# A fused attention and two-MLP kernel: the softplus table's place, B and C stored without zeros, and an early order planned with eight transfers in flight

## The chip, the cores and the metric

One core of one Trainium2 chip runs the program. The metric is device time in microseconds (us), the median of three runs. Engines: PE is TensorE (matmuls), ACT ScalarE, DVE VectorE, POOL GpSimd; SP is SyncE, which here only issues transfers (its queue is SPq).

## The reference

Three stages follow each other. Stage 1 is a linear attention with decay (4 sequences, 8 heads, 768 positions, head size 32, state size 16):

```python
log_a = np.log(np.clip(a, 1e-06, 1.0))
cum = np.cumsum(la, axis=-1)                       # per chunk
M = einsum(C, B) * exp(cum_i - cum_j) * causal
y = M @ x + (C @ state) * exp(cum)
state = decay_full * state + sum_j B_j x_j decay_from_j
```

Stage 2 (MLP 1) and stage 3 (MLP 2) each take 3072 tokens of 256 features through 2048 hidden features and back:

```python
h = x @ w_in
g = np.maximum(h, 0.0) + np.log1p(np.exp(-np.abs(h)))      # stage 2: softplus
g = np.where(h >= 1, h, np.where(h <= -1, 0, (h + 1)**2/4)) # stage 3
out = (g @ w_out).astype(np.float32)
```

The MLP weights come as 64-bit floats and are put together from their 32-bit halves on the chip.

## The kernel before

**Tiling.** The 768 positions are six blocks of 128 (c = 0 to 5). A block of all four sequences (b = 0 to 3) gives 512 tokens. An MLP step s is one `up(s)` (128 hidden features for 512 tokens, in a PSUM bank h or z), the activation `g(s)` and one `down(s)` (into two accumulators). The first four steps do block 0 in halves: 256 tokens and two feature groups each. Precise products are made of a high part and a low part of each factor: `up` is six matmuls (`wih` with `xh`, `wil` with `xh`, `wih` with `xl`, for two halves of the 256 features). A `down` of the first WHOLE = 8 steps takes `g` and the 32-bit weight `w32` undivided; later ones take `g_hi`, `g_lo` and split weights (`woh`, `wol`) in six matmuls.

**The way of a weight.** A weight piece (kind i or o, number j; 512 KB) is loaded into a staging buffer `st0` to `st3`, or, for j = 2, `raw` (`load_w`, L780). From its two halves it is made: `w0` (the upper half, scaled; on ACT, or DVE), `w1` (the lower half's bits, on ACT with Relu), `w2` and, for weights whose sign `w0` hasn't taken, `w3` (both on DVE). PRELU says how many i and o pieces get their sign in `w0`, by a Prelu on ACT. `w_hi` casts to `wih` or `woh`, `split_w` (L966) makes `wil` or `wol` on DVE or POOL.

**Attention, block 0.** ACT makes eight exponentials (`decay`, L1125), POOL the products `bt` (`sources`, L1131), PE the `scores` of B and C (L1170), DVE `weigh` (L1179), PE `out` for each sequence (L1236, L1257), ACT and DVE `xh` and `xl` (`evac` L1289, `ready` L1297). `up(0)` and `up(1)` need sequences 0 and 1, `up(2)` and `up(3)` the other two.

**B and C.** A pair of sequences of a block comes as one tile `bc` of 128 x 768 numbers (384 KB), a third B and two thirds C; half of the C part is zeros, so that one matmul gives two heads apart.

**What sets the order.** `Jobs.order` is a planner: each job has an engine, a cost, needs and buffers; the planner takes jobs one by one by start and due time, and the code is written out in that order. Every engine then does its instructions strictly in that order, each waiting for what it needs. ACT holds one table of functions at a time: exp, ln and Prelu first, softplus after a table load, which stands inside `g(0)` at L1421. Where the planner sees PE idle in the first 26 us, matmuls on a tile of zeros are put in (L1545, "idle"); LULL = 5 of them stand before `down(0)`. In SP's queue each issue also waits until the eighth one before it has landed, so no more than eight transfers are in flight.

Of the kernel before, what the change touches and what calls it, by code (L numbers as in the profile page):

```python
# [15 lines left out]
Q = 128  # L16
# [11 lines left out]
class Jobs:  # L28
# [18 lines left out]
    def order(self, slots, begin):  # L47
# [29 lines left out]
        pipe = 0.0  # L77
# [23 lines left out]
        for _ in range(len(jobs)):  # L101
# [142 lines left out]
def program():  # L244
# [23 lines left out]
    add("clip_a", DVE, 380, needs=["a_load"])  # L268
    add("log", ACT, 260, needs=["clip_a"])
# [6 lines left out]
    add("clip_load", SP, 400, due=-1e5, size=98e3)  # L276
    add("clip", DVE, 350, needs=["clip_load", ("columns", 1)] + [("rows_of", b) for b in range(NB - 1)])
# [3 lines left out]
    for c in range(1, NC):  # L281
        add(("store_runs", c), ACT if c == 1 else SP, 450 if c == 1 else 600, needs=[("runs", 1)], size=16e3)
        add(("dec", c), ACT if c == 1 else SP, 600 if c == 1 else 400, needs=[("store_runs", i) for i in range(1, NC if c > 1 else 2)], takes=["dec"], size=262e3)
    for u in range(NU):
        c, b = divmod(u, NB)
        if u % 2 == 0:
            add(("load_bc", u // 2), SP, 400, takes=["bc"], size=393e3)
        add(("load", u), SP, 400, takes=["u"], size=262e3)
# [162 lines left out]
    for s, (m, c, t0, n, fc, m_fc) in enumerate(steps):  # L451
# [30 lines left out]
        if m == 0:  # L482

            add(
                ("g", s), ACT, 500 if s else 1850, needs=[made] + [("decay", b, hg) for b in range(NB * (s == 0)) for hg in range(2)]
                + [("w0", 0, kind, j) for kind in "io" for j in range(8 * (s == 0)) if signed(0, kind, j)],
# [37 lines left out]
    result = jobs.order(slots, {POOL: 3700, ACT: 2000, PE: 5500, DVE: 2500, SP: 900})  # L524
# [6 lines left out]
WHOLE = 8  # L531
# [16 lines left out]
PRELU = (2, 2)  # L548
LOW_ACT = 1
LOW_DVE = set()  # L550
PRE_FROM = 3
BIAS = {DVE: 400, POOL: 500}
# [25 lines left out]
    ("cd", 7): -1000, ("decay", 5): -16000, ("load_w", 1, "i", 2): -16000, ("w1", 0, "o", 1): 16000, ("weigh", 2, 0): -16000,  # L578
}
WARM = 10  # L580
LULL = 5
# [6 lines left out]
def tile_kernel(ctx: ExitStack, tc: tile.TileContext, a0, al, bc, ub, w_in, w_out, w2_in, w2_out, out):  # L588
# [486 lines left out]
    def load_bc(engine, v):  # L1075

        nc.sync.dma_start(mine("load_bc", v)[0], bc[v])
# [521 lines left out]
```

## Time and profile before

| | |
|---|---|
| runs | 555.07, 555.45, 555.97 us (median 555.45) |
| the profiled execution | 555.7 us, of which its span is 553.9 us |
| PE busy | 547.3 us, 99% of the span |
| DVE, ACT, POOL busy | 437.5, 391.1, 38.8 us |
| moved by DMA | 64.73 MB |

The profile's times run from the span's start. A row of the timeline gives the start and the duration of an instruction, or of several alike that are merged, and in brackets how long its engine sat idle before it, and what ended that. Instructions of one engine overlap a little at their ends, so the distance of two starts is often shorter than a duration.

### The profile page before, as it was taken

To read this page: it belongs to the slowest core of one execution; us is meant where nothing else is said; L and a number is where in the kernel's file an instruction comes from. 1 tells how busy PE (TensorE), PEld (TensorE's weight loads), DVE (VectorE), ACT (ScalarE), POOL (GpSimd) and SP (SyncE) were. 2 spreads that over 40 slices of the span, in tenths; PEclk is the share of its full clock that TensorE was granted. 3 is DMA by queue.
4 is the path that set the end of the run, shared out by engine and by line. 5 is a ranking of instruction groups with operands and counts; after the bars stand their busy time and mean duration, and the time that the engine had idled before them with its cause. 6 is when DMAs were issued, how large, how long until landed. Compare 5 with 4: busy or idle time off the path is not lost.

```text
span 553.9 us, 10465 instructions
## 1 busy us (share of the span) xinstructions
PE 547.3 (99%) x4001; PEld 442.8 (80%) x4001; DVE 437.5 (79%) x817; ACT 391.1 (71%) x719; POOL 38.8 (7%) x44
## 2 busy tenths in 40 slices
PE   9999999999999999999999999999999999999997
PEld 4777878888888888888888888888888888888885
DVE  7889899798856899876687898989886665876663
ACT  7969655636456667665666989786988875988783
POOL 4023110000000100001300000021310000000000
PEclk9999999999999999999999999999999999999999
DMA  7996458567232500376337324514100001100002
GB/s 271 392 238 198 130 179 235 165 213 219 90 133 76 181 1 1 113 253 227 111 116 233 108 77 145 179 38 149 44 1 0 2 0 38 39 0 1 1 1 76
DMA packets 34679, 64.73 MB, mean 117 GB/s; under 512 B 3684, under 2 KB 8164, under 8 KB 34628
## 3 DMA queue, kind: packets, MB, share of 16 engines
q1 hardware_dynamic: 34276, 63.65, 35.8%
q8 instruction: 31, 0.51, 0.4%
q10 hardware_dynamic: 352, 0.41, 0.3%
q14 instruction: 20, 0.16, 0.1%
HBM read 47.61 MB, written 16.43 MB: 116 GB/s over the span
## 4 chain that ended last, share of the span: by engine, by line
PE 93%; DMA 2%; DVE 2%; ACT 1%; SPq 1%; issue 1%; DVEq 0%; ACTq 0%
PE acc L1463 45%; PE h L1334 5%; PE h L1335 5%; PE h L1336 5%; PE z L1334 4%; PE z L1335 4%; PE z L1336 4%; PE h L1327 4%; PE h L1329 4%; PE h L1328 4%; PE acc L1451 3%; PE y L1236 1%; DMA st<-in_w_in_dram 1%; PE y L1268 1%; DMA u<-in_ub_dram 1%; PE z L1329 1%
## 5 line engine op out<-in xcount | busy, mean ns | idle before, releaser
L1437 DVE TENSOR_TENSOR gl<-g,gh 128x512 fp32r<-128x512 f32 x182 | 127.5, 705 | 55.0 <-PE acc L1463 31.1
L1463 PE MATMUL acc<-gh,woh 128*128 128x512 f32 x368 | 144.3, 392 | 0.0
L1463 PE MATMUL acc<-gh,wol 128*128 128x512 f32 x368 | 143.3, 389 | 0.0
L733 ACT CAST gh<-g 128x512 fp32r<-128x512 f32 x171 | 106.2, 621 | 26.4 <-PE acc L1463 14.2
L1463 PE MATMUL acc<-gl,woh 128*128 128x512 f32 x368 | 113.5, 389 | 0.0
L1463 PEld LDWEIGHTS acc<-gh,woh 128*128 128x128 f32 x368 | 69.1, 188 | 15.3 <-issue 0.7
L1463 PEld LDWEIGHTS acc<-gl,woh 128*128 128x128 f32 x368 | 69.1, 188 | 14.4
L1463 PEld LDWEIGHTS acc<-gh,wol 128*128 128x128 f32 x368 | 69.1, 188 | 14.1
L1422 ACT ACTIVATE g<-h 128x512 f32<-128x512 f32 x61 | 36.5, 598 | 52.5 <-PE h L1329 36.6
L1414 ACT ACTIVATE t<-t 128x512 f32<-128x512 f32 x96 | 60.9, 634 | 1.9
L1327 PE MATMUL h<-xh,wih 128*128 128x512 f32 (+1 forms) x114 | 45.8, 402 | 0.0
L1328 PE MATMUL h<-xh,wil 128*128 128x512 f32 (+1 forms) x114 | 42.8, 376 | 0.0
L1329 PE MATMUL h<-xl,wih 128*128 128x512 f32 (+1 forms) x114 | 42.8, 376 | 0.0
L1123 DVE TENSOR_TENSOR_SCAN ld<-ld,eye_t 128x512 f32<-128x512 f32 x20 | 26.5, 1364 | 2.2 <-DMA ld<-clip_z 2.2
L1407 ACT ACTIVATE t<-h 128x512 f32<-128x512 f32 x37 | 22.1, 598 | 7.5 <-PE h L1336 6.5
L1426 DVE TENSOR_TENSOR g<-h,t 128x512 f32<-128x512 f32 x37 | 25.3, 685 | 1.1 <-ACT t L1414 0.3
L1407 ACT ACTIVATE t<-z 128x512 f32<-128x512 f32 x35 | 21.0, 599 | 7.1 <-DVE g L1426 3.9
L1327 PEld LDWEIGHTS h<-xh,wih 128*128 128x128 f32 x114 | 21.5, 188 | 5.3 <-issue 1.1
L1426 DVE TENSOR_TENSOR g<-z,t 128x512 f32<-128x512 f32 x35 | 24.0, 686 | 1.5 <-ACT t L1414 0.5
L1328 PEld LDWEIGHTS h<-xh,wil 128*128 128x128 f32 x114 | 21.4, 188 | 4.6 <-issue 0.7
L1329 PEld LDWEIGHTS h<-xl,wih 128*128 128x128 f32 x114 | 21.4, 188 | 4.1
L1422 ACT ACTIVATE g<-z 128x512 f32<-128x512 f32 x19 | 11.4, 598 | 17.0 <-PE z L1336 8.5
(326 smaller groups left out, 1011.5 us busy)
## 6 DMA issues: line engine op xcount, KB each, us to landing
st<-in_w_in_dram SPq DMA_DIRECT2D x15, 512.0 KB, 5.2
st<-in_w_out_dram SPq DMA_DIRECT2D x15, 512.0 KB, 6.3
u<-in_ub_dram SPq DMA_DIRECT2D x24, 256.0 KB, 6.6
ld<-clip_z SPq DMA_DIRECT2D x20, 256.0 KB, 6.2
bc<-in_bc_dram SPq DMA_DIRECT2D x12, 384.0 KB, 5.7
pre_i<-st_plain SPq DMA_DIRECT2D x15, 256.0 KB, 2.0
pre_s<-st_plain SPq DMA_DIRECT2D x14, 192.0 KB, 5.9
pre_o<-st_plain SPq DMA_DIRECT2D x10, 256.0 KB, 2.5
```

Of the source, the lines that this page charges most:

```text
L733: nc.scalar.copy(out, in_)
L1327: nc.tensor.matmul(o, wh, xh[c][:, k, t0:t0 + n], start=(k == 0), stop=False)
L1328: nc.tensor.matmul(o, wl, xh[c][:, k, t0:t0 + n], start=False, stop=False)
L1329: nc.tensor.matmul(o, wh, xl[c][:, k, t0:t0 + n], start=False, stop=(k == 1))
L1334: nc.tensor.matmul(bank, wh, bh, start=start, stop=False, skip_group_check=True)
L1335: nc.tensor.matmul(bank, wl, bh, start=False, stop=False, skip_group_check=True)
L1336: nc.tensor.matmul(bank, wh, bl, start=False, stop=True, skip_group_check=True)
L1414: nc.scalar.activation(out=t, in_=t, func=AF.Square, scale=0.5 / SAT, bias=0.5)
L1422: nc.scalar.activation(out=g, in_=ph, func=AF.Softplus)
L1426: nc.vector.tensor_tensor(out=g, in0=ph, in1=t, op=ALU.max)
L1437: engines[engine].tensor_tensor(out=mine("g_lo", s)[0], in0=mine("g", s)[0], in1=mine("g_hi", s)[0].bitcast(F32), op=ALU.subtract)
L1463: nc.tensor.matmul(acc_t(s, e), w, g[:, j * n:(j + 1) * n], start=(begins(e, j) and g is gh and i == 0), stop=(fc + j == NFC - 1 and g is ...
```

## The change

- `table` becomes a job of its own. It needs block 0's eight exponentials and the Prelu weights, and no longer stands inside `g(0)`.
- B and C of a pair of sequences are stored as 128 rows of 512 numbers, in two halves by row parity, with no zeros. Two transfers of 64 x 512 load them, each into the columns where its rows have data. The places of the zeros in the three `bc` buffers are cleared once (`clear`: two on DVE, one on POOL). The matmuls of `scores` read the same columns in a strided way.
- The planner holds SP until the eighth transfer back has landed. Costs of a few jobs are set anew, and so are numbers that steer the order.
- PRELU (2, 2) becomes (2, 1): piece (o, 1) gets its sign by `w3`. Eight `w1` move from ACT to DVE (LOW_DVE). WHOLE 8 becomes 7, LULL 5 becomes 1.

```diff
+                lands += [end + self.LATENCY[SP]] * (2 if cost >= 800 else 1)
+                clock[SP] = max([clock[SP]] + lands[-8:-7])
...
+    add("table", ACT, 1280, needs=[("decay", b, hg) for b in range(NB) for hg in range(2)]
+        + [("w0", 0, kind, j) for kind in "io" for j in range(8) if signed(0, kind, j)])
...
-            add(("load_bc", u // 2), SP, 400, takes=["bc"], size=393e3)
+            add(("load_bc", u // 2), SP, 800, takes=["bc"], size=262e3 if u else 170e3)
...
-                ("g", s), ACT, 500 if s else 1850, needs=[made] + ...
+                ("g", s), ACT, 500, needs=[made] + ["table"] * (s == 0),
...
-WHOLE = 8
+WHOLE = 7
-PRELU = (2, 2)
+PRELU = (2, 1)
-LOW_DVE = set()
+LOW_DVE = {(0, 'i', 6), (0, 'i', 2), (0, 'i', 5), (0, 'o', 7), (0, 'i', 7), (0, 'o', 0), (0, 'o', 6), (0, 'i', 0)}
-BIAS = {DVE: 400, POOL: 500}
+BIAS = {DVE: 300, POOL: 500}
-LULL = 5
+LULL = 1
...
     def load_bc(engine, v):
-        nc.sync.dma_start(mine("load_bc", v)[0], bc[v])
+        t = mine("load_bc", v)[0].rearrange("(r e) f -> e r f", e=2)
+        for e in range(2):
+            nc.sync.dma_start(t[e][:, 256 * e:256 * e + 512], bc[v, e])
...
+    def table(engine):
+        nc.scalar.preload_act_table_set("softplus")
...
+    def clear(engine, i):
+        engine.memset(buf("bc", i).rearrange("r (k f) -> r k f", k=3)[:, 0:3:2], 0.0)
```

**ACT from the first `s0` copy to `g(0)`.** `w32<-st1` is `w0` of weight (o, 0), `st2` holds (i, 1), `st3` (o, 1); `t<-` and `g<-` are `w1`; `gh<-h1` is `g(0)`. Before:

```order
L1289 CAST xh0_360<-y1_266 128x2x128
L1291 COPY s0_66<-y1_266 128x64
L794 ACTIVATE w32_383<-st1_137 128x512
L804 ACTIVATE t_387<-st1_137,low_bias_73 128x512
L794 ACTIVATE w32_327<-st2_138 128x512
L804 ACTIVATE t_406<-st3_139,low_bias_73 128x512
L794 ACTIVATE w32_383<-st3_139 128x512
L804 ACTIVATE g_412<-st2_138,low_bias_73 128x512
L1421 ACT_TABLE_LOAD
L1422 ACTIVATE gh_415<-h1_210 128x512
```

Now, the same stretch of ACT:

```order
L797 ACTIVATE w32_368<-st1_137 128x512
L736 CAST wih0_74<-w32_331 128x512
L1294 CAST xh0_362<-y1_267 128x2x128
L1296 COPY s0_66<-y1_267 128x64
L797 ACTIVATE w32_331<-st2_138 128x512
L807 ACTIVATE t_392<-st2_138,low_bias_73 128x512
L1423 ACT_TABLE_LOAD
L807 ACTIVATE t_431<-st3_139,low_bias_73 128x512
L1429 ACTIVATE gh_434<-h1_212 128x512
```

One ACT instruction on `st3` instead of two stands ahead of `g(0)`, and it stands behind the table load; the cast of `wih0` has come to ACT, ahead of sequence 1's `xh0`.

**SP's queue at the start.** Before:

```order
L992 DMA first_241<-in_a0_dram 128x1x128
L1077 DMA bc0_243<-in_bc_dram 128x768
L1038 DMA more0_148<-in_al_dram 48x512
L1082 DMA u0_130<-in_ub_dram 128x512
L1082 DMA u1_131<-in_ub_dram 128x512
L780 DMA st0_136<-in_w_in_dram 128x2x512
L1077 DMA bc1_249<-in_bc_dram 128x768
L1082 DMA u2_132<-in_ub_dram 128x512
L1082 DMA u3_133<-in_ub_dram 128x512
L780 DMA st1_137<-in_w_out_dram 128x2x512
L780 DMA st2_138<-in_w_in_dram 128x2x512
L780 DMA st3_139<-in_w_out_dram 128x2x512
```

Now:

```order
L995 DMA first_247<-in_a0_dram 128x1x128
L1082 DMA bc0_208<-in_bc_dram 64x512 x2
L1041 DMA more0_148<-in_al_dram 48x512
L1087 DMA u0_130<-in_ub_dram 128x512
L1087 DMA u1_131<-in_ub_dram 128x512
L1082 DMA bc1_243<-in_bc_dram 64x512 x2
L783 DMA st0_136<-in_w_in_dram 128x2x512
L1087 DMA u2_132<-in_ub_dram 128x512
L1087 DMA u3_133<-in_ub_dram 128x512
L783 DMA st1_137<-in_w_out_dram 128x2x512
L783 DMA st2_138<-in_w_in_dram 128x2x512
L783 DMA st3_139<-in_w_out_dram 128x2x512
```

Both `bc` loads are two transfers each, and the second pair has moved ahead of the first weight piece.

**POOL after its first `bt` products.** Before:

```order
L1131 TENSOR_TENSOR bt2_325<-u2_132,ld2_120 128x64 x2
L1131 TENSOR_TENSOR bt3_366<-u3_133,ld3_121 128x64 x2
L966 TENSOR_TENSOR wol0_98<-w32_383,woh0_90 128x512
L966 TENSOR_TENSOR wol1_99<-w32_383,woh1_91 128x512
L966 TENSOR_TENSOR wil6_88<-w32_650,wih6_80 128x512
```

Now:

```order
L1136 TENSOR_TENSOR bt2_328<-u2_132,ld2_120 128x64
L1136 TENSOR_TENSOR bt3_349<-u3_133,ld3_121 128x64
L969 TENSOR_TENSOR wil0_82<-w32_331,wih0_74 128x512
L969 TENSOR_TENSOR wol0_98<-w32_368,woh0_90 128x512
L969 TENSOR_TENSOR wol4_102<-w32_622,woh4_94 128x512
```

`wil0`, which `up(0)` needs, has come from DVE to POOL, as its first weight. On PE the first products follow each other as before; of the matmuls on zeros, 15 stood between the first `out` and `down(0)` before (1, 2, 7 and 5 in a row) and 9 do now (2, 6 and 1); the seven behind `up(0)` are gone. Block 1's `scores` have moved from behind the ninth `down` to behind the sixth.

## Rows read from the trace of the kernel before

**Rows 1.** The page: busy times, and the clock in 40 slices.

```profile
PE 547.3 (99%) x4001; PEld 442.8 (80%) x4001; DVE 437.5 (79%) x817; ACT 391.1 (71%) x719; POOL 38.8 (7%) x44
...
PEclk9999999999999999999999999999999999999999
```

**Rows 2.** Waits of PE, 20 us to the end: total, times, longest.

```profile
PE acc L1451 <- ACT gh L1422: 0.9, 1, 0.9
PE y L1236 <- DVE ld L1179: 0.5, 1, 0.5
```

**Rows 3.** Timeline of PE, 13 to 22 us: start, duration, what, count.

```profile
13.95 0.38 PE L1328 MATMUL h<-xh,wil 128*128 128x256 f32 x1
...
15.59 1.69 PE L1545 MATMUL y<-idle 128*128 128x512 bf16 x7
...
17.20 0.64 PE L1236 MATMUL y<-ld,u 128*32 128x128 f32 x16
...
18.44 1.25 PE L1545 MATMUL acc<-idle 128*128 128x512 bf16 x5
...
20.58 1.99 PE L1451 MATMUL acc<-gh,w 128*128 128x256 f32 x8 [0.89 <-ACT gh L1422]
...
22.22 0.47 PE L1327 MATMUL h<-xh,wih 128*128 128x256 f32 x1
```

**Rows 4.** Timeline of ACT, 13 to 20 us.

```profile
13.20 0.41 ACT L1289 CAST xh<-y 128x256 fp32r<-128x256 f32 x1
...
13.45 0.27 ACT L1291 COPY s<-y 128x64 f32<-128x64 f32 x1
...
13.83 0.67 ACT L794 ACTIVATE w<-st 128x512 f32<-128x512 f32 x1
...
14.40 0.75 ACT L804 ACTIVATE t<-st,low_bias 128x512 uint32<-128x512 uint32 x1
...
16.59 0.77 ACT L804 ACTIVATE t<-st,low_bias 128x512 uint32<-128x512 uint32 x1 [0.71 <-DMA st<-in_w_out_dram]
...
17.85 0.77 ACT L804 ACTIVATE g<-st,low_bias 128x512 uint32<-128x512 uint32 x1
...
18.64 1.28 ACT L1421 ACT_TABLE_LOAD   x1
...
19.93 0.60 ACT L1422 ACTIVATE gh<-h 128x512 f32<-128x512 f32 x1
```

**Rows 5.** Timeline of SP's queue: three issues that waited for st1, st2, st3.

```profile
13.88 0.33 SPq L1082 DMA_DIRECT2D u<-in_ub_dram  x1
...
15.23 0.38 SPq L780 DMA_DIRECT2D st<-in_w_in_dram  x1
...
16.58 0.34 SPq L1082 DMA_DIRECT2D u<-in_ub_dram  x1
```

**Rows 6.** Timeline of POOL: the first two weights that it splits.

```profile
27.94 1.53 POOL L966 TENSOR_TENSOR wol<-w,woh 128x512 fp32r<-128x512 f32 x1 [13.89 <-ACT woh L733]
...
35.47 1.28 POOL L966 TENSOR_TENSOR wol<-w,woh 128x512 fp32r<-128x512 f32 x1 [6.00 <-ACT woh L733]
```

**Rows 7.** Timeline of DVE: 128x512 on one operand, and on two.

```profile
20.20 0.42 DVE L792 TENSOR_SCALAR w<-raw 128x512 f32<-128x512 f32 x1
...
22.71 0.69 DVE L828 SCALAR_TENSOR_TENSOR w<-raw,w 128x512 uint32<-128x512 uint32 x1
```

**Rows 8.** The chain that ended last: an undivided and a split down.

```profile
34.83 1.72 PE acc L1451 x4
...
48.64 1.36 PE acc L1463 x6
```

**Rows 9.** Busy time by stretch: PE, PEld, DVE, ACT, POOL, clock, DMA share, GB/s.

```profile
40.00:50.00 10.00, 10.00 (x45) 6.62 (x46) 10.00 (x21) 8.36 (x16) 0.00 (x0) 1.00 0.66 206
...
552.00:553.90 1.90, 0.00 (x0) 0.00 (x0) 0.00 (x0) 0.00 (x0) 0.00 (x0) 0.58 0.34 119
```

**Rows 10.** Timeline of PE: block 2's out.

```profile
77.33 0.80 PE L1236 MATMUL y<-ld,u 64*32 64x64 f32 x60 [0.48 <-DVE ld L1179]
```

More of the change, by code (lines that the diff above doesn't have):

```diff
@@ L76, in order @@
         clock = {engine: begin.get(engine, 0.0) for engine in self.LATENCY}
-        pipe = 0.0
+        pipe, lands = 0.0, []
         ready = {name for name in jobs if missing[name] == 0}
@@ L267, in program @@
     add("a_load", SP, 400, due=-2e5, takes=["g"], size=66e3)
-    add("clip_a", DVE, 380, needs=["a_load"])
-    add("log", ACT, 260, needs=["clip_a"])
+    add("clip_a", DVE, 50, needs=["a_load"])
+    add("log", ACT, 120, needs=["clip_a"])
     add("sums", DVE, 350, needs=["log"])
@@ L281, in program @@
     for c in range(1, NC):
-        add(("store_runs", c), ACT if c == 1 else SP, 450 if c == 1 else 600, needs=[("runs", 1)], size=16e3)
-        add(("dec", c), ACT if c == 1 else SP, 600 if c == 1 else 400, needs=[("store_runs", i) for i in range(1, NC if c > 1 else 2)], takes=["dec"], size=262e3)
+        add(("store_runs", c), ACT if c == 1 else SP, 450 if c == 1 else 600, needs=[("runs", 1)], size=620e3 if c == 1 else 16e3)
+        add(("dec", c), ACT if c == 1 else SP, 600 if c == 1 else 400, needs=[("store_runs", i) for i in range(1, NC if c > 1 else 2)], takes=["dec"], size=560e3 if c == 1 else 262e3)
     for u in range(NU):
@@ L286, in program @@
         if u % 2 == 0:
-            add(("load_bc", u // 2), SP, 400, takes=["bc"], size=393e3)
-        add(("load", u), SP, 400, takes=["u"], size=262e3)
+            add(("load_bc", u // 2), SP, 800, takes=["bc"], size=262e3 if u else 170e3)
+        add(("load", u), SP, 400, takes=["u"], size=262e3 if u else 354e3)
         if c == 0:
@@ L484, in program @@
             add(
-                ("g", s), ACT, 500 if s else 1850, needs=[made] + [("decay", b, hg) for b in range(NB * (s == 0)) for hg in range(2)]
-                + [("w0", 0, kind, j) for kind in "io" for j in range(8 * (s == 0)) if signed(0, kind, j)],
+                ("g", s), ACT, 500, needs=[made] + ["table"] * (s == 0),
                 takes=["gh" if whole(s) else "g"], gives=[frees],
@@ L523, in program @@
     slots = dict(sx=2, h=2, y=2, z=0, acc=4, t=2, g=N_G, gh=4, gl=3, ld=3, lp=2, u=4, bc=3, bt=BT, dec=2, st=2, st2=1, st3=1, w32=5, cs=2)
-    result = jobs.order(slots, {POOL: 3700, ACT: 2000, PE: 5500, DVE: 2500, SP: 900})
+    result = jobs.order(slots, {POOL: 3700, ACT: 2000, PE: 5440, DVE: 2500, SP: 900})
     a, b = (next(i for i, r in enumerate(result) if r[0] == name) for name in ("clip_load", ("load_bc", 0)))
@@ L1570 @@
     by_g = lambda v: v.reshape(NB // 2, 2, 2, 2, 2, NC, Q, N).transpose(5, 0, 1, 2, 4, 7, 3, 6)
-    cz = np.zeros((NC, NB // 2, 2, 2, 2, N, 2, 2, Q), x.dtype)
-    for e in range(2):
-        cz[:, :, :, :, e, :, :, e] = by_g(C.reshape(NB, H, NC, Q, N))[:, :, :, :, e]
-    late = cz[1:].reshape(NC - 1, NB // 2, 2, 2, 2, N, 2, 2, 2, HALF)
-    cz[1:] = late.transpose(0, 1, 2, 3, 4, 5, 6, 8, 7, 9).reshape(cz[1:].shape)
-    bc = np.ascontiguousarray(np.concatenate(
-        [by_g(B.reshape(NB, H, NC, Q, N)).reshape(NU // 2, 128, 256), cz.reshape(NU // 2, 128, 512)], axis=2
+    bg, cg = (by_g(v.reshape(NB, H, NC, Q, N)).reshape(NU // 2, 4, 2, N, 256).transpose(2, 0, 1, 3, 4).reshape(2, NU // 2, 4 * N, 256) for v in (B, C))
+    bc = np.ascontiguousarray(np.stack(
+        [np.concatenate([cg[0], bg[0]], axis=2), np.concatenate([bg[1], cg[1]], axis=2)], axis=1
     ))
```

18 lines of the change are left out of this document (10 added, 8 removed).

## Prediction

> **What bounds the kernel now.** First the busy times: PE is at work 547.3 of 553.9 us [rows 1], so the only ways to gain are to start its long run of work sooner, to make that run shorter, or to remove waits inside it. The waits of PE from 20 us on are two, 0.9 and 0.5 us [rows 2]. The first stands right in front of `down(0)`, at 20.58 [rows 3]. From there the chain is PE's own work (a `down`, an `up`, a `down`) to the end, but for the 0.48 us in front of block 2's `out` [rows 10]. So what `down(0)` gains, the kernel gains, as long as everything that PE takes later still comes in time.
>
> What sets 20.58 is read backwards on ACT [rows 4]: `g(0)` starts at 19.93, right after the table load (18.64 for 1.28). In front of that stand `w1` of `st2` (17.85), one `w0`, and `w1` of `st3` at 16.59, for which ACT had sat idle 0.71 us. That wait ended with a landing: SP's issues at 13.88, 15.23 and 16.58 are those that wait for `st1`, `st2` and `st3` [rows 5], so these landings are known to a few hundredths. The chain is thus: `st3` lands at 16.58, three ACT instructions, the table, `g(0)`. PE had its own part done earlier: `up(0)` runs until the seven matmuls on zeros at 15.59, the last two `out` from 17.20 to 18.44, then five more on zeros [rows 3]. About 3 us of PE's time here are zeros and waiting.
>
> **The change part by part.**
>
> Bytes. A `bc` tile falls from 128 x 768 to 128 x 512 numbers of 4 bytes: 131 KB less each. Two of them stand before `st1`, 262 KB. One weight piece (524 KB) lands every 1.35 us [rows 5], 388 KB per us, so the three landings move 0.68 us forward: 13.20, 14.55, 15.90. The two added issues cost SP some 0.35 us each [rows 5], but SP at this point only waits for landings, with transfers queued behind each other. If this cover is gone, the landings stay where they are; that end is kept below.
>
> ACT, in the new order. `w0` of `st1` at 13.20; the cast of `wih0` 0.57 later (13.83 to 14.40 is that step [rows 4]) at 13.77; 0.60 for the cast, as the 128x512 of `g(0)` has [rows 4]: `xh0` of sequence 1 at 14.37; 0.25 (13.20 to 13.45): `s0` at 14.62; 0.25: `w0` of `st2` at 14.87 (landed); 0.57: `w1` of `st2` at 15.44; 0.79 (17.85 to 18.64): the table at 16.23; 1.29 (18.64 to 19.93): `w1` of `st3` at 17.52, long landed; 0.79: `g(0)` at 18.31. It ends at 18.91, and `down(0)` can start 0.05 later as before: 18.96. The table load now stands where ACT would otherwise wait for `st3` or do work for later.
>
> PE, in the new order. `up(0)` needs `wil0`, which POOL makes now. `wih0` is there at 14.37; POOL's two rows of this shape are 1.53 and 1.28 us [rows 6], so `wil0` comes at 15.7 to 15.95. DVE made it in 0.69 [rows 7]; what POOL adds is paid by the seven zeros that are gone. From the second matmul of `up(0)` to its end is 1.64 us (13.95 to 15.59), the two `out` 1.24 (17.20 to 18.44), one matmul on zeros 0.25 (1.25 for five) [rows 3]: `down(0)` could start at 18.85 to 19.1. The two chains meet; I take 19.0, so 1.6 us sooner than 20.58. Bounds: with both chains at their best, 18.75; with the old landings, ACT and PE are 0.68 later, 19.7.
>
> WHOLE 8 to 7. The eighth `down` becomes six split matmuls, 1.36 instead of 1.72 us [rows 8]: 0.36 us less on PE, on the path. It adds one cast and one difference, on engines with room at that place (below).
>
> Work for DVE. Three clears of 512 numbers a partition, no row shows one; the nearest, 128x512 on one operand, is 0.42 [rows 7]. One stands on DVE before SP's first `bc`, one before the clipping of `a`, one is on POOL. I count them at nothing, since ACT reaches the wait for `st1` with about 0.8 us to spare (one `w1` and one pair of `xh` and `s0` less stand ahead of it); without that cover they cost up to 0.4. Eight `w1` of 0.42 and one `w3` of 0.69 come to DVE [rows 7]; five casts and two `w0` of 0.42 go from it to ACT in the order: +1.1 us in all, spread over the first 70 us. ACT loses eight `w1` and gains seven, shorter, instructions.
>
> What is late next. `up(1)` starts at 20.64 (`down(0)` takes 1.64, 20.58 to 22.22 [rows 3]). Its `wih1` is on ACT 0.50, 0.25 and 0.25 after `g(0)`, hence 19.3 to 19.9, `wil1` on DVE 0.69 later, 20.6 to 20.7: in time, or a tenth late. I found nothing behind it that is due as tightly. Block 2's `out` keeps its wait: in both orders the same matmuls stand between the end of block 1's `out`, which frees the buffers for block 2's decays, and block 2's. I keep the 0.48.
>
> Sum: 555.7 (profiled execution) - 1.6 - 0.36 = 553.7. The median of the runs is 0.25 below the profiled one: **553.5 us**. The forecast's own range is 552.8 (0.25 more at the start, the 0.48 gone) to 554.3.
>
> **The rivals.**
>
> The transfers don't come sooner. Smaller and more transfers may keep fewer bytes on the way, and the table, whatever its name says, still stands behind `w0` of `st2`, so behind a landing. Then `down(0)` starts at 19.7: 555.45 - 0.9 - 0.36 = 554.2, and 554.6 if POOL is slower than its rows. For it: the early issues are many. Against: the rate of the landings is steady [rows 5]. 0.12.
>
> DVE becomes the bound. It is busy 10.00 of 10 us from 40 to 50 [rows 9]. If it can't follow, PE waits at block 2's `out` for what it had won: 555.5, and 556.5 if the added 1.1 us come on top. Against: DVE's work for block 2 starts from block 1's `out`, which moves with PE, and block 1's part stands three steps earlier in the order. 0.12. A stall of another kind that the new order makes later, 1 to 3 us: 0.06, 554.5 to 556.5.
>
> The clock falls; the case that ends slower. Six zeros fewer stand ahead of `down(0)`, and PE now stands still for over a microsecond inside `up(0)`, until `wil0` comes. The granted clock is full in all slices [rows 1], through a wait of 0.89 us [rows 3], and lower only after the last matmul, 0.58 on average from 552 us on [rows 9]. [...] 0.05. [...]
>
> A switch of tables costs more than its load. If a drain came with it, `g(0)` would be later by it. The rows show none: `w1` ends at 18.62, the load starts at 18.64, and `g(0)` 0.01 after its end [rows 4]. A drain as long as the load itself, 1.28 us, would put `down(0)` at 20.3 and the time at 554.8. 0.03. [...]
>
> **How the numbers follow.** The forecast has 0.62, the rivals 0.12, 0.12, 0.06, 0.05 and 0.03. Faster by over 0.2% (under 554.34; about what a measurement of this kernel can tell from no change) are the forecast and half of the first rival, less a little for a run of POOL that is slow: 0.67. Within 0.2%: the other half, most of DVE's case, the drain, most later stalls: 0.23. Slower: the clock, and the ends of DVE's case and of the later stalls: 0.10. The range 552.8 to 555.6 leaves out the clock, the worse half of DVE's case, a part of the later stalls, and a few hundredths below.
>
> **What would show it.** `down(0)` at 18.75 to 19.3, no ACT wait for `st3` in front of the table, the table near 16.2, `w0` of `st1` near 13.2. Eight undivided `down` become seven. PE's waits after that stay at some 0.5 us. It is wrong if the landings didn't move, if POOL's `wil0` takes clearly over 1.5 us, if the granted clock shows a dip between 14 and 21 us, or if new waits of PE for DVE add up to over 1 us.

## The result, and the profile after

The changed kernel takes **557.95 us** (median of seven runs, 556.49 to 560.80), the kernel before 555.07 on the same chip: 1.0051 times the time, 95% interval 1.0030 to 1.0073. It is 2.9 us slower, where 1.95 us of gain had been forecast, and lies outside the range.

The page of the changed kernel, against [rows 1]: PE has about as much to do as before, DVE 7.4 us more, nearly all of it behind 140 us (127.7 instead of 124.0 from 140 to 300, 82.8 instead of 78.5 from 430 on), where no wait of PE is listed. In the first 80 us, where the loss arises, DVE is busy for 0.7 us more.

```profile
PE 546.8 (98%) x3997; PEld 443.5 (80%) x3997; DVE 444.9 (80%) x830; ACT 387.6 (70%) x715; POOL 33.9 (6%) x41
```

Its waits of PE (total, times, longest), against [rows 2]; the one at L1505 stands ahead of all work, and the kernel before has one like it. The two in `up(0)` are new, the one in front of `down(0)` is gone, and block 2's `out`, 0.5 us before, now costs 2.9.

```profile
PE y L1241 <- DVE ld L1184: 2.9, 1, 2.9
PE h L1505 <- DVE idle L1502: 1.1, 1, 1.1
PE h L1332 <- ACT xh L1294: 0.7, 1, 0.7
PE h L1333 <- POOL wil L969: 0.7, 1, 0.7
```

The start, on PE's timeline, against [rows 3]: `up(0)` runs from 15.56 to about 18.1, block 0's last sums from 18.16, one matmul on zeros, and `down(0)` at 19.62, 0.96 sooner than 20.58.

```profile
15.56 0.38 PE L1332 MATMUL h<-xh,wih 128*128 128x256 f32 x1 [0.73 <-ACT xh L1294]
16.66 0.38 PE L1333 MATMUL h<-xh,wil 128*128 128x256 f32 x1 [0.71 <-POOL wil L969]
...
18.16 0.64 PE L1241 MATMUL y<-ld,u 128*32 128x128 f32 x16
...
19.40 0.39 PE L1558 MATMUL acc<-idle 128*128 128x512 bf16 x1
19.62 1.89 PE L1458 MATMUL acc<-gh,w 128*128 128x256 f32 x8
```

ACT's timeline there, against [rows 4]. ACT waits 1.31 us for the output weight's tile `st1`, which comes at 14.06; the table load is at 16.86; behind it there is no wait.

```profile
14.06 0.67 ACT L797 ACTIVATE w<-st 128x512 f32<-128x512 f32 x1 [1.31 <-DMA st<-in_w_out_dram]
...
15.52 0.68 ACT L797 ACTIVATE w<-st 128x512 f32<-128x512 f32 x1
16.09 0.76 ACT L807 ACTIVATE t<-st,low_bias 128x512 uint32<-128x512 uint32 x1
16.86 1.28 ACT L1423 ACT_TABLE_LOAD   x1
18.16 0.81 ACT L807 ACTIVATE t<-st,low_bias 128x512 uint32<-128x512 uint32 x1
18.87 0.58 ACT L1429 ACTIVATE gh<-h 128x512 f32<-128x512 f32 x1
```

Then block 2. What its `out` takes is made in a chain: SP loads rows into the buffers that block 1's `out` frees (at 52.0 here, at 61.6 before), DVE makes the decays of them in four scans, and weighs them with the scores. SP's queue: the four row transfers are issued at 52.15, right behind a weight of 512 KB. In the kernel before, the last weight had been issued 2.3 us sooner (59.41).

```profile
51.68 0.37 SPq L783 DMA_DIRECT2D st<-in_w_out_dram  x1
52.15 3.15 SPq L1098 DMA_DIRECT2D ld<-clip_z  x4
```

The same transfers before:

```profile
61.69 3.38 SPq L1093 DMA_DIRECT2D ld<-clip_z  x4
```

DVE's timeline: the four decay scans start at 59.26 and take 7.84 us; before, they start at 67.54 and take 6.63.

```profile
59.26 7.84 DVE L1128 TENSOR_TENSOR_SCAN ld<-ld,eye_t 128x512 f32<-128x512 f32 x4 [1.09 <-DMA dec<-clip_p]
```

```profile
67.54 6.63 DVE L1123 TENSOR_TENSOR_SCAN ld<-ld,eye_t 128x512 f32<-128x512 f32 x4 [0.86 <-DMA ld<-clip_z]
```

POOL's timeline: three low halves of `g` are made beside them; before, there were two (67.40 for 3.46).

```profile
59.24 1.30 POOL L1444 TENSOR_TENSOR gl<-g,gh 128x512 fp32r<-128x512 f32 x1 [12.75 <-PE acc L1470]
61.99 1.83 POOL L1444 TENSOR_TENSOR gl<-g,gh 128x512 fp32r<-128x512 f32 x1 [1.45 <-ACT gh L736]
64.72 1.30 POOL L1444 TENSOR_TENSOR gl<-g,gh 128x512 fp32r<-128x512 f32 x1 [0.90 <-ACT gh L736]
```

```profile
67.40 3.46 POOL L1437 TENSOR_TENSOR gl<-g,gh 128x512 fp32r<-128x512 f32 x2 [12.12 <-PE h L1329]
```

PE's timeline, against [rows 10], and the stretches behind it (the last three numbers are granted clock, DMA share, GB/s): after 2.9 us without work, PE goes on at half the clock until 74.

```profile
70.26 0.96 PE L1241 MATMUL y<-ld,u 64*32 64x64 f32 x58 [2.89 <-DVE ld L1184]
```

```profile
70.00:71.00 1.00, 0.74 (x64) 0.74 (x67) 1.00 (x3) 0.00 (x0) 0.00 (x0) 0.77 0.00 0
71.00:73.00 2.00, 2.00 (x90) 1.73 (x71) 2.00 (x9) 0.42 (x1) 0.00 (x0) 0.50 0.04 8
73.00:74.00 1.00, 1.00 (x4) 0.72 (x4) 1.00 (x4) 1.00 (x5) 0.00 (x0) 0.52 0.00 0
74.00:76.00 2.00, 2.00 (x13) 1.37 (x15) 2.00 (x5) 0.34 (x2) 0.00 (x0) 1.00 0.00 0
```

The profiled execution adds up: 0.96 sooner at `down(0)`, 0.36 less for the eighth `down`, which became split, 2.41 more at block 2's `out` (2.89 for 0.48), and about 1.3 for the half clock (the sums behind the wait take 1.86 us instead of the 1.41 of e10 below, and the next four matmuls 1.86 instead of 1.04). That is 2.4 more; the span is 556.2 for 553.9, 2.3 more.

### The profile page after: what moved, and what is told of

Same layout as the page of the kernel before. It is cut to its first block, busy times and chain, and to the rows that moved or that the text cites. A ratio compares the mean times of both kernels' runs of the same rounds, so it can differ in the third digit from the quotient of the medians.

```text
span 556.2 us, 10474 instructions
## 1 busy us (share of the span) xinstructions
PE 546.8 (98%) x3997; PEld 443.5 (80%) x3997; DVE 444.9 (80%) x830; ACT 387.6 (70%) x715; POOL 33.9 (6%) x41
## 4 chain that ended last, share of the span: by engine, by line
PE 95%; DMA 2%; ACT 1%; DVE 1%; SPq 0%; issue 0%; POOL 0%
PE acc L1470 45%; PE h L1332 5%; PE h L1339 5%; PE h L1340 5%; PE h L1341 5%; PE h L1333 4%; PE h L1334 4%; PE z L1339 4%; PE z L1340 4%; PE z L1341 4%; PE acc L1458 2%; PE y L1241 2%; DMA st<-in_w_out_dram 1%; PE y L1273 1%; PE z L1332 1%; PE z L1333 1%
## 5 line engine op out<-in xcount | busy, mean ns | idle before, releaser
L736 ACT CAST gh<-g 128x512 fp32r<-128x512 f32 x169 | 104.8, 620 | 23.1 <-PE acc L1470 13.2
L1470 PEld LDWEIGHTS acc<-gh,wol 128*128 128x128 f32 x370 | 69.5, 188 | 14.2
```

What stands on the lines that cost most here:

```text
L736: nc.scalar.copy(out, in_)
L1470: nc.tensor.matmul(acc_t(s, e), w, g[:, j * n:(j + 1) * n], start=(begins(e, j) and g is gh and i == 0), stop=(fc + j == NFC - 1 and g is ...
```

## The experiments

All times are medians, with the ratio (and its 95% interval) to the kernel before, run beside them on the same chip: its own median lay between 554.75 and 555.65, so ratios are what is compared. In the diffs, `shift(a, b)` puts job a right behind job b in the finished order and `on(a, E)` gives it to engine E; nothing else is moved by them. A job's name has its step, its weight or its sequence: `g_lo` is the low half of a `g`, `sm` readies a block's states, `st` makes its sums on PE, and sequence 11 is the last of block 2.

**Block 2's wait.** The first four take the wait of 2.9 us apart.

```diff
+on(("g_lo", 11), DVE); shift(("g_lo", 11), ("decay", 11))
+on(("g_lo", 12), DVE); shift(("g_lo", 12), ("weigh", 11, 1))
+on(("g_lo", 13), DVE); shift(("g_lo", 13), ("cd", 11))
```

> Edit to the changed kernel: the low halves of g for steps 11, 12 and 13, which POOL makes (59.24 for 1.30 us, 61.99 for 1.83, 64.72 for 1.30), are made on DVE instead, step 11's behind block 2's four decay scans, the other two behind the weighing. Theory A (POOL beside the scans): the four scans take about 4 x 1.20 = 4.8 us instead of 7.84, one low half of 0.69 stands behind them, so the weighing ends about 2.3 us sooner; PE's wait at block 2's out falls from 2.9 to about 0.6 us, the clock stays at 1.00 behind it (about 1.6 us more), and the time is about 3 to 4 us under the changed kernel's, near 554. Theory B (DVE simply has too much work since more of the weights' steps are its own): three more operations of 0.69 us on DVE make it worse; wait of 3.5 us or more, time 0.5 to 2 us over the changed kernel's.

556.80 us, 1.0022 (1.0008 to 1.0036). The scans take 4.57 us, no wait is left at block 2's `out`, and the clock stays at 1.00. Theory A holds in mechanism; of the 3 to 4 us about 1.6 came (from 1.0051 to 1.0022), and B is out. DVE's timeline of e1:

```profile
60.39 4.57 DVE L1143 TENSOR_TENSOR_SCAN ld<-ld,eye_t 128x512 f32<-128x512 f32 x4 [0.73 <-DMA ld<-clip_z]
```

The views of that line, of the kernel before, the changed kernel, and e1 (shortest, median, longest of the four, in ns): beside POOL's low halves one of these scans takes 2.23 to 2.36 us, alone 1.20.

```profile
L1123 DVE TENSOR_TENSOR_SCAN ld<-ld,eye_t x4: 1191/1713/2242, 67.5 to 73.0; 128x512 f32<-128x512 f32 x4
```

```profile
L1128 DVE TENSOR_TENSOR_SCAN ld<-ld,eye_t x4: 1194/2259/2360, 59.3 to 64.8; 128x512 f32<-128x512 f32 x4
```

```profile
L1143 DVE TENSOR_TENSOR_SCAN ld<-ld,eye_t x4: 1197/1198/1226, 60.4 to 63.8; 128x512 f32<-128x512 f32 x4
```

```diff
+shift(("load_w", 0, "o", 7), ("load", 11))
+shift(("w0", 0, "o", 7), ("g_hi", 13))
```

> Edit to the changed kernel: the load of output weight 7, issued at 51.68 just ahead of block 2's rows, is issued behind block 2's four u loads, and its first step on ACT is moved back behind the g of step 13. Theory A (the 512 KB of the weight stand ahead of the rows): the scans start about 1.3 us sooner (58.0 instead of 59.26, though not before DVE's own work ends at about 58.2), the scans still take about 7.8 us, the wait at block 2's out is about 1.6 to 1.9 us instead of 2.9; time 1 to 2.5 us under the changed kernel's, the more the less the clock falls. Rival (the rows are late because of something else, the start is DVE's own): scans start within 0.3 us of 59.26 and the time is within 0.3 us of the changed kernel's.

556.77 us, 1.0023 (1.0008 to 1.0038). With the weight behind them, the rows are issued at 52.77 and the scans start at 58.76, 6.0 us later (7.1 in the changed kernel, 6.75 in e1, which has the weight ahead too, and 5.85 before); here DVE has no idle time before them. PE waits 1.62. So the load ahead lengthened this way by 0.8 to 1.1 us. That the scans take 6.67 us here is luck: POOL's third low half falls beside two multiplications behind them (1.57 us instead of 0.46). PE's timeline of e2; the clock stays at 1.00 behind it.

```profile
69.69 0.80 PE L1252 MATMUL y<-ld,u 64*32 64x64 f32 x60 [1.62 <-DVE ld L1195]
```

```diff
+shift(("st", 11), ("up", 19))
```

> Edit to the changed kernel: on PE alone, block 2's sums (its out and states) are moved behind the next first matmul of the layer (step 19's, 2.7 us of work that hangs on g of step 17 only). DVE, ACT, POOL and the transfers keep their order. Theory A (what is lost is PE's idle time and the clock behind it, both from one wait): PE waits about 0.9 us for the bank instead of 2.9, the granted clock stays at 1.00 and the time is 3 to 3.6 us under the changed kernel's, near 554.4. Rival (the block's chain is late anyway and what is saved here is lost where block 2's states are next wanted): the 2 us come back as a wait at the sums and carries behind it, and the time is within 1 us of the changed kernel's.

557.87 us, 1.0041 (1.0029 to 1.0053). The wait fell to 1.61 and the clock stayed (0.999 on average over the profiled run), but new waits of 1.34 us at 46 and 0.48 at 79 stand in the profile: the rival's result, though the one at 46 lies ahead of the edit.

```diff
+            if name == ("st", 11):
+                for i in range(9):
+                    nc.tensor.matmul(buf("h", 0)..., idle, ..., start=True, stop=True)
```

> Edit to the changed kernel: nine matmuls of zeros of 512 columns are put ahead of block 2's out on PE, into the bank that the next step overwrites; they hang on g of step 17 (about 68.2) and last about 2 us, so that PE has nothing to do for about 0.9 us instead of 2.9, while its useful work goes on at the same 70.26. The wait itself is kept. Theory A: the granted clock stays at 1.00 behind the gap, where the changed kernel has 0.50 to 0.77 for 3.2 us; the time is about 1.6 us under the changed kernel's. Rival (the clock's fall costs nothing, since DVE sets the end of this stretch): within 0.3 us of the changed kernel's, with PE's clock at 1.00 and a new wait of about 1.5 us on DVE behind it.

558.63 us, 1.0059 (1.0042 to 1.0076). The clock is 1.00 in every stretch, as asked for, and nothing is gained: in e4 a g at 33 came 1.03 us late. So keeping the clock alone doesn't bring the time down. Why the median is this high is not shown: the profiled execution, 557.76, is the second fastest of six. Both e3 and e4 differ from the changed kernel before their edit has any effect, so the stretch from 30 to 50 us must itself vary from one execution to the next.

**Where it varies.** In e1's profile, ACT waits for weights that haven't landed (1.85 us to 32.13, 0.75 to 44.25), with a g behind them. The kernel before has one such wait from 20 to 60 us, of 0.4 us; the changed one has four, of 4.6 in all.

```diff
+shift(("g", 4), ("sm", 3))
+shift(("g", 7), ("up", 7)); shift(("g_hi", 7), ("g", 7))
```

> Edit: the kernel of e1_low_dve (low halves of steps 11, 12, 13 on DVE), and on ACT the g of step 4 stands ahead of the two first steps of input weight 4, and g and its cast of step 7 ahead of those of input weight 6, so that neither stands behind an activation that waits for a weight's landing. Nothing else moves. Theory C (second cause of the loss: in the changed order ACT reaches a weight before it has landed, 1.85 and 0.75 us of wait in e1's profile at 30.3 and 43.5, and a g that is ready stands behind it): PE's gaps of 0.58 ahead of the fourth step's second matmul (33.4) and of 0.56 at the low half of step 7 (47.4) go, the time is about 1.2 us under e1's, 555.6. Rival (these gaps come from PE's own bank order or from the transfers themselves): the gaps stay within 0.2 us and the time is within 0.3 us of e1's.

557.01 us, 1.0039 (1.0025 to 1.0052), no better than e1. The two gaps went and others came: 0.74 at block 1's states (50.2), 0.65 at block 2's `out`. Theory C is right on the gaps and wrong on the gain. The timelines of e5 show where the gap at 50.2 comes from: four multiplications that last 0.28 each elsewhere take 4.19 us beside POOL's three weight splits.

```profile
43.79 4.19 DVE L1166 TENSOR_TENSOR u<-u,dec 128x128 f32<-128x128 f32 x4
```

```profile
43.75 3.88 POOL L987 TENSOR_TENSOR wol<-w,woh 128x512 fp32r<-128x512 f32 x3 [6.10 <-ACT woh L754]
```

```diff
+for j in (0, 1, 2, 4): on(("split_w", 0, "o", j), DVE)   # four lines
+shift(("split_w", 0, "o", 4), ("g_lo", 7)); shift(("split_w", 0, "o", 0), ("carry", 11))
+shift(("split_w", 0, "o", 1), ("split_w", 0, "o", 0)); shift(("split_w", 0, "o", 2), ("w2", 0, "o", 7))
```

> Edit: the kernel of e5_g_ahead, and the four low halves of output weights 0, 1, 2 and 4, which POOL makes between 33 and 48 us (3.9 to 4.5 us for the first, some 4 us for the other three), are made on DVE, weight 4's behind the low half of g of step 7, the others behind block 2's carries and later. POOL then has nothing to do between 17 and 80 us. Theory A' (POOL beside DVE costs DVE far more than POOL's own share of the work): in e5's profile four multiplications of 128x128 at 43.8 last 4.19 us beside POOL, where those of block 2 last 0.28 each; they fall to 0.9 to 1.1 us, the first decay scan of block 1 to 1.2 us; the gap of 0.74 us at block 1's states and that of 0.65 at block 2's out go; the time is 1.4 to 2 us under e5's, about 555.3. Rival (DVE has too much work in this stretch): four operations of 0.68 us more on DVE keep a gap of 0.5 us or more at block 2's out, and the time is within 0.4 us of e5's.

556.21 us, 1.0012 (1.0004 to 1.0020): 1.5 us better than e5 by ratio, as Theory A' said. The gap at block 1's states is gone, but the one at block 2's `out` is not (0.78 us, where Theory A' had none). The profiled execution, 557.94, is the slowest of twelve. The multiplications are back to 0.89 for four:

```profile
45.29 0.89 DVE L1174 TENSOR_TENSOR u<-u,dec 128x128 f32<-128x128 f32 x4
```

A new wait of 1.64 us for a g stands at 77. e11 adds e2's edit and input weight 0's low half on DVE:

```diff
+shift(("load_w", 0, "o", 7), ("load", 11)); shift(("w0", 0, "o", 7), ("g_hi", 13))
+on(("split_w", 0, "i", 0), DVE)
```

> Edit: the kernel of e9_no_pool, with the output weight 7 loaded behind block 2's u loads (as in e2_weight_behind) and the low half of input weight 0 on DVE instead of POOL (1.28 us there, 0.68 on DVE). Theory A': no gap over 0.2 us is left between 20 and 80 us; the second matmul of the first up starts about 0.6 us sooner, the first down no more than 0.3 us sooner, since the first g waits for weight tiles on ACT; the time is that of the changed order without its waits, 553.5 to 554.6, under the kernel before (about 555). Rival (the changed order has DVE at its limit): a gap of 0.5 us or more stays somewhere from 40 to 76 us, time 555 to 557.

556.52 us, 1.0020 (1.0009 to 1.0031): the rival, and no faster than e9. Behind `down(0)` one wait of over 0.25 us is left, 1.12 at 75.5, for g of step 19, whose buffer a low half on DVE frees late, because e9's splits were put ahead of it.

```diff
+shift(("g_lo", 16), ("carry", 11))
+shift(("split_w", 0, "o", 0), ("w3", 0, "o", 7))       # was ("carry", 11)
+shift(("split_w", 0, "o", 1), ("ready", 11))           # was behind weight 0
+shift(("split_w", 0, "o", 2), ("g_lo", 14))            # was ("w2", 0, "o", 7)
```

> Edit: the kernel of e11_all_four with DVE's order changed behind block 2: the low half of g of step 16 stands right behind block 2's carries, and the three low halves of output weights 0, 1 and 2 stand behind it, ahead of the steps that use them. Theory: the 1.12 us that PE waits at 75.5 for g of step 19 (whose buffer that low half frees) goes, no gap over 0.3 us is left behind the first down; the time is 1 to 1.3 us under e11's, 555.2 to 555.5, equal to the kernel before or just under. Rival (DVE is at its limit from 57 to 80 us): the wait moves to another place of the stretch and the time is within 0.4 us of e11's.

555.13 us, 0.9993 (0.9985 to 1.0002): level with the kernel before, and 3.2 us below the changed one (0.9993 against 1.0051). The theory holds, though the wait in `up(0)` stays. PE's waits in e13; behind `down(0)` only 0.6 us is left, in three pieces:

```profile
PE h L1363 <- DVE wil L999: 0.8, 1, 0.8
PE h L1362 <- ACT g L1459: 0.6, 3, 0.2
PE h L1362 <- ACT xh L1324: 0.4, 1, 0.4
```

**The transfers of B and C.** e6 gives the kernel before the new form alone, e7 the changed kernel the old form.

```diff
-        nc.sync.dma_start(mine("load_bc", v)[0], bc[v])
+        for e in range(2):
+            nc.sync.dma_start(t[e][:, 256 * e:256 * e + 512], bc[v, e])
```

> Edit to the kernel before: only the new form of B and C (two transfers of 128 KB without zeros for each pair in place of one of 384 KB with them, and the three clears), in the order of before. Theory D (bytes, the step of the prediction): the 262 KB fewer ahead of the output weight's tile let it land about 0.65 us sooner, 13.2 instead of 13.9, and the two tiles behind it likewise; the first down starts about 0.6 us sooner; time about 0.5 us under the kernel before. Rival E (the form itself: each half costs SP 0.56 us of issue, and the stream at 8 to 12 us runs at 230 to 330 GB/s instead of 400): the tile lands at 13.7 to 14.4, the first down starts within 0.3 us of 20.6 or later, time from the same to 0.8 us over.

557.88 us, 1.0053 (1.0036 to 1.0071). ACT takes the tile at 12.97, without a wait for it, and `down(0)` starts at 19.16, 1.4 sooner: theory D for the start, though not for the time. But input weight 5, issued at 37.34 instead of 35.18, comes late, a g stands behind it on ACT, PE waits 1.95 us at 42.7, and the granted clock falls to 0.50 (46 to 48 us). ACT's timeline of e6:

```profile
41.52 0.77 ACT L804 ACTIVATE t<-st,low_bias 128x512 uint32<-128x512 uint32 x1 [4.37 <-DMA st<-in_w_in_dram]
```

> Edit to the changed kernel: B and C are loaded as before (one transfer of 384 KB with the zeros, no clears), in the changed order. Theory D (bytes): the output weight's tile lands about 0.65 us later than the changed kernel's 14.06, at 14.7, and the first down starts 0.3 to 0.6 us later; time 0.3 to 0.8 us over the changed kernel's. Rival E (the halves cost what their bytes save): it lands at 13.6 to 14.2 and the time is the changed kernel's within 0.4 us or better. Either way PE's wait of about 2.9 us at block 2's out stays, since the order is the changed one's.

558.69 us, 1.0069 (1.0052 to 1.0085). The tile came at 13.28, sooner than the changed kernel's 14.06: rival E for the start. The time is 1 us over the changed kernel's by ratio, which the intervals can't tell from none. By these two profiles e6 and e7 contradict each other on bytes; the comparison over all runs is below.

```diff
+        if v > 1:
+            nc.sync.dma_start(mine("load_bc", v)[0], bcz[v])   # with zeros, as before
+            return
```

> Edit to the kernel before, in its own order: only the first two pairs of B and C are loaded in two transfers without zeros (262 KB fewer ahead of the first weights), all later pairs as before in one with zeros. Theory G (e6's early gain is the bytes; its later loss is the doubled transfers, each of which holds one of eight places: the trace of before has each transfer issued when the eighth before it lands): the output weight's tile lands at 13.0 to 13.3 instead of 13.9, the first down starts at 19.2 to 19.9 instead of 20.6, no weight lands late at 41, and the time is 0.6 to 1.3 us under the kernel before. Rival (the order of before has no slack at 36 to 50 us, whoever starts it sooner): as in e6, a wait of 1 us or more for g near 42, and the time 1 to 3 us over the kernel before.

556.47 us, 1.0020 (1.0008 to 1.0032). `down(0)` at 19.72, and a wait of 1.78 us at 43.2: the rival. Here it is output weight 5, 3.00 us late, with the g of step 7 behind it. So the order of before has no slack there either: start it sooner, and the weights at 40 us are late. Moving that g ahead of the late weights gives e14 (from e12) and e15 (from e6):

```diff
+shift(("g", 7), ("up", 7))
```

> Edit to the kernel of e12_bc_first_two (order of before, first two pairs of B and C without zeros): g of step 7 stands on ACT right behind the g of its first matmul's turn, ahead of the four steps of input weight 5 and output weight 5, the second of which waited 3.00 us there for its landing. Theory G' (the 1.78 us at 43.2 are that g standing behind a late weight): the wait at 43.2 is under 0.3 us, the early gain of 0.9 us stays, and the time is 1 to 1.9 us under e12's, 554.6 to 555.4, under the kernel before by up to 0.9. Rival (the weight itself is what PE needs next): a wait of 1 us or more comes back at the following matmuls, and the time is within 0.5 us of e12's.

555.75 us, 1.0011 (1.0000 to 1.0023). The wait at 43.2 is gone and 0.5 us won by ratio, within the intervals, but the time is not under that of the kernel before: in this profile the early gain was 0.35 only (`down(0)` at 20.23), and a new wait of 0.54 stands at 55.

> Edit to the kernel of e6_bc_alone (order of before, all pairs without zeros): the same move of g of step 7. Theory G': the wait of 1.95 us at 42.7 and the clock's fall behind it go, the early gain of 1.4 us stays, the time is 2.5 to 3.5 us under e6's, 554.4 to 555.4. Rival (the doubled transfers hold places and the weights land later still than in e12): input weight 5, which landed at 41.5 there against 38.9 in the kernel before, is what the next first matmuls wait for; a wait of 1 us or more stays and the time is 556 to 558.

557.96 us, 1.0040 (1.0027 to 1.0053): the rival. PE waits 1.03 us at 47.1 for the cast of an input weight itself.

**The table.**

```diff
+shift("table", ("w1", 0, "o", 1))
```

> Edit to the changed kernel: the load of the softplus table stands where it stood before, right ahead of the first g (behind the first step of output weight 1); nothing else moves. Theory F (the early table hides under a wait for the last weight tile): the first g and the first down come 0.5 to 0.7 us later, at 20.1 to 20.3 instead of 19.6, and the time is 0.5 us over the changed kernel's. Rival F' (there is no such wait left: by the profile the tile that the step behind the table wants had landed before the table's load began): the first down moves by less than 0.2 us and the time stays within 0.3 us of the changed kernel's.

557.95 us, 1.0043 (1.0031 to 1.0055): the changed kernel's time. Rival F' holds: from `st1` to `g(0)` ACT takes 4.83 us, and 4.81 in the changed kernel. (`down(0)` starts at 18.73, since `st1` came at 13.17 in this profile.) ACT's timeline of e10: the two steps at 15.19 run into each other, so the tile that the table was to be hidden under was there by 15.95, and g starts right behind the table.

```profile
13.17 0.67 ACT L807 ACTIVATE w<-st 128x512 f32<-128x512 f32 x1 [0.95 <-DMA st<-in_w_out_dram]
14.63 0.68 ACT L807 ACTIVATE w<-st 128x512 f32<-128x512 f32 x1
15.19 1.50 ACT L817 ACTIVATE t<-st,low_bias 128x512 uint32<-128x512 uint32 x2
16.71 1.28 ACT L1433 ACT_TABLE_LOAD   x1
18.00 0.60 ACT L1439 ACTIVATE gh<-h 128x512 f32<-128x512 f32 x1
```

e8 tried the early table in the kernel before.

```diff
-            if s == 0:
-                nc.scalar.preload_act_table_set("softplus")
+("table", ACT) behind ("w0", 0, "i", 1)
```

> Edit to the kernel before: only the load of the softplus table is moved, from inside the first g to just behind the first step of input weight 1 on ACT, ahead of the step that waits for the last weight tile; everything else as before. Theory F (the table takes the place of a wait): ACT waits 0.71 us there for the tile's landing, so 0.7 of the table's 1.28 us is hidden, the first g and the first down start 0.7 us sooner (19.9 instead of 20.6) and the time is 0.5 to 0.7 us under the kernel before. Rival: the tile is there by then or the first down waits for the five matmuls of zeros or a low half of the weight instead; the first down moves by less than 0.2 us and the time is the same within 0.2 us.

558.51 us, 1.0062 (1.0047 to 1.0077). Neither theory is tried by this: a Prelu of output weight 1 stands behind the new place there and wants the first table back, so two more loads of 1.28 us came. In the change, that weight gets its sign on DVE.

```profile
16.20 1.28 ACT L1429 ACT_TABLE_LOAD   x1
...
18.30 1.28 ACT L805 ACT_TABLE_LOAD   x1
...
20.92 1.28 ACT L1435 ACT_TABLE_LOAD   x1
```

**The first up.** e16 and e17 start from e13 and take the tile `st1` out of the way of `up(0)`; e16 also has the low half `wil0` back on POOL, e17 keeps it on DVE.

```diff
+shift(("w0", 0, "o", 0), ("evac", 1))
+shift(("g", 0), "table")
+shift(("w2", 0, "i", 1), ("w2", 0, "o", 0))
```

> Edit: the kernel of e13_gl_sooner, with the low half of input weight 0 back on POOL, and three moves at the first up: on ACT the cast of input weight 0 and block 0's second cast stand ahead of output weight 0's first step (which waits 1.2 us for its tile there), the first g stands right behind the table, ahead of output weight 1's step, and on DVE output weight 0 is finished ahead of input weight 1. Theory H (the first up waits for a tile that it doesn't use, since its operands' casts stand behind that tile's step on ACT): the first matmul starts at 15.1 behind the zeros, the second without a wait of over 0.2 us, the first down at 18.7 to 18.9 instead of 19.55; the time is 0.5 to 0.8 us under e13's, 554.4 to 554.7, under the kernel before by some 0.8. Rival (POOL's 1.28 us beside DVE's weighing, or the weighing itself, sets block 0's last sums): the first down moves by less than 0.3 us and the time is e13's within 0.3 us.

554.85 us, 0.9987 (0.9977 to 0.9998). `up(0)` runs without a wait, `down(0)` starts at 18.77, though the tile came at 14.20 in this profile. Theory H holds for the start; of the 0.5 to 0.8 us under e13, 0.3 came by ratio, which the intervals can't tell from none. The time is 0.7 us under the kernel before by ratio, the interval just short of 1, and 3.5 under the changed one.

> Edit: as e16_first_up_pool, with the low half of input weight 0 on DVE (0.68 us) as in e13_gl_sooner. Theory H: the second matmul of the first up at about 15.7, block 0's last sums at 17.3 to 17.5, since their weighing comes 0.6 us later on DVE than in e16, the first down at 18.7 to 19.0; time within 0.3 us of e16's. If POOL beside DVE's weighing costs DVE more than its own 0.68 us would, this one is the faster, by up to 0.4 us.

555.06 us, 0.9988 (0.9977 to 0.9999), `down(0)` at 19.13: level with e16.

## Why the prediction was wrong, step by step

**The landings (the forecast's first term): failed.** `st1` was to land 0.68 us sooner, at 13.20, for 262 KB fewer bytes. It came at 14.06. The issue that follows its landing stands at 13.22 to 14.53 in the twelve profiles with the changed order and the new form (the changed kernel, e1 to e5, e9 to e11, e13, e16, e17), mean 13.92; in the kernel before it is 13.88. The spread of 1.3 us between executions is twice the term, and the mean shows no gain. I took one execution's landings "to a few hundredths" as if they were fixed. The added issues were also put too low, at 0.35 us each: a pair of halves takes SP 1.16 and 1.12 us where one load took 0.41 and 0.47, and `st1` is issued at 7.17 instead of 5.51. In the kernel before, 10 to 14 us moved 395 to 408 GB/s; in the changed kernel 9 to 12 us moved 231 to 277. In the order of before, the bytes did tell: with the new form `st1` lands by 12.4 (e6), 12.95 (e12), 13.5 (e14) and 13.1 us (e15), with the old form by 13.9 (the kernel before) and 14.2 (e8), although the new form's issue stands at 7.1 there too. In the changed order the second pair is issued ahead of the first weight `st0`, whose issue so comes at 5.54 instead of 4.38 (e6). That this took the gain is not shown; the one profile of the changed order with the old form (e7, 13.4) lies within the spread of the twelve.

**ACT's and PE's chains: right.** From `st1` to `g(0)` ACT was to take 5.11 us and took 4.81 (6.10 before); POOL made `wil0` in 1.28. With the landing 0.86 later than forecast, `down(0)` came at 19.62 instead of 19.0: 0.96 of the 1.6 us. PE's chain was the later one: `g(0)` had ended at 19.45.

**The table: right place, wrong reason.** I had it stand where ACT "would otherwise wait for `st3` or do work for later". e10 shows no such wait: its place is worth nothing. What shortened the chain were the steps taken out of it.

**WHOLE: as forecast in count** (44 of those matmuls for 48, so seven undivided `down`), and the sum above has room for its 0.36. It was not tried alone.

**"Block 2's `out` keeps its wait": failed, and it decides.** The argument was that the same matmuls stand between block 1's `out` and block 2's. They do: 15.4 us (52.0 to 67.4) against 15.3 (61.6 to 76.9). But the chain beside them, transfers and DVE, grew from 15.7 us to 18.2: the weight issued ahead of the rows, 0.8 to 1.1 of it by e1 and e2 (from issue to scans 7.1 us instead of 5.85), and a third POOL operation beside the scans, about 1.2 (scans of 7.84 us instead of 6.63; in e1, with none, 4.57). "I found nothing behind it that is due as tightly" was a look at `up(1)` alone. Two things of the trace of before told of it: the 0.48 us [rows 10] mean that this chain had no slack at all, and POOL's two low halves there already lay beside two slow scans.

**DVE's added work at nothing: wrong in part.** The 1.1 us of more operations, 0.7 of busy time in the first 80 us, matter less than where POOL stands beside them.

**The rivals.** "The transfers don't come sooner", at 0.12, came true for the start: it had `down(0)` at 19.7, and it was 19.62. Its time, 554.2, did not, for the wait at block 2. "DVE becomes the bound" named the place, at 0.12, and priced it at what had been won and 1.1 us at most, 556.5; the wait grew by 2.4 us, 1.1 more than the 1.3 won (0.96 and 0.36), and the half clock came on top. The clock fell, but behind block 2's wait, not in `up(0)`, where gaps of 0.73 and 0.71 us left it at 1.00. What a fall costs, no row of the trace before shows; behind block 2's wait the granted clock went to 0.50, and that cost about 1.3 us. The drain stayed away: the load ends at 18.14 and the next step starts at 18.16.

**What was missed as a whole** is that a new order is a new set of waits. By e13 and e16, nearly every wait behind `down(0)` had been removed, one by one, and each showed the next: the start's gain is real, but the stretch from 25 to 80 us runs at the edge of transfers, ACT and DVE in either order (e12, e14). By the sum, e13 and e16 should lie a further 1 us lower. From the start of `down(0)` to the start of PE's last matmul, less the waits listed, are 528.45 us before (20.58 to 549.51, less 0.48) and 529.15 in e13 (19.55 to 549.32, less 0.62), where 0.36 less was due. Most of this is in the short waits themselves, which cost more than is listed: the list counts from the end of a matmul of 0.39 us, though the next one elsewhere starts 0.23 us behind its start, and the step behind a wait is longer too. At e13's first wait two steps take 0.89 us (70.09 to 70.98) instead of 0.46, so 0.43 is lost where 0.17 is listed; its three waits come to 1.4 us that way. Some 0.3 us stay open.

```profile
69.86 0.39 PE L1363 MATMUL h<-xh,wil 128*128 128x512 f32 x1
70.09 0.39 PE L1364 MATMUL h<-xl,wih 128*128 128x512 f32 x1
70.64 0.50 PE L1362 MATMUL h<-xh,wih 128*128 128x512 f32 x1 [0.17 <-ACT g L1459]
70.98 0.40 PE L1363 MATMUL h<-xh,wil 128*128 128x512 f32 x1
```

## What to carry to other kernels

A wait of half a microsecond that PE has behind a chain of other engines means that chain has no slack: when PE's work ahead of it is moved, cost the whole chain anew, transfers and the other engines' neighbours too. In an in-order queue, put what is ready ahead of what waits for a landing, since landings differ by a microsecond from one execution to the next (13.22 to 14.53 above). Before POOL is given work, look at what DVE does beside it (a scan of 2.23 to 2.36 us instead of 1.20 above).

## What the runs showed of the hardware that I had not expected

**POOL beside DVE.** Some DVE operations took longer while POOL worked. With both operands in SBUF: a scan 2.23 to 2.36 us (the kernel before and the changed one) instead of 1.20 (e1), four small multiplications 4.19 (e5) instead of 0.89 (e9). With one operand, in SBUF too: a cast of 128x512 in the kernel before, 1.39 at 28.36 beside POOL's split (27.94 for 1.53), where its other casts of this shape have medians of 0.41 to 0.43. Others did not, even with both operands in SBUF: in the changed kernel a scan at 35.11 took 1.22 while POOL's split ran (33.55 for 3.87). Nor did the weighings looked at, which have one operand in PSUM: in e16 two take 1.28 us from 13.38, the second of them beside POOL's split (13.86 for 1.27), and in e17 two take 0.68 each from 16.03, with POOL idle.

```profile
13.38 1.28 DVE L1216 TENSOR_TENSOR ld<-acc,ld 128x512 f32<-128x512 f32 x2
```

**The clock's fall is not settled by the gap's length alone.** Behind gaps of PE of 2.89 us (the changed kernel), over 2.2 (e7), 2.85 (e8) and 1.95 (e6) the granted clock fell from 1.00 to 0.50; behind 2.89 in the profiled execution of e10 and 1.78 in e12 it stayed at 1.00. What decides between the two is not shown.

The mean granted clock of a whole run tells of the runs without a profile. In the profiled runs it is 0.996 or 0.997 where the clock fell, and 0.998 or more where it did not. By that, it fell in four of the changed kernel's seven runs (557.95 to 560.80 us; the other three took 556.49 to 557.54), in four of e10's five, in one of e2's twelve and in none of e4's six. So the four longest runs of the changed kernel are those with a fall, but the fall does not settle its median: e4 is no faster without one.
